# A hand-ordered attention and gated-MLP kernel: the same 8,030 operations replayed in another order

## The chip, the core and the metric

The kernel runs on one core of a Trainium2 chip. The metric is the device time of one execution in microseconds (us). Three runs of the kernel before took 676.34, 678.39 and 679.76 us; the median, 678.39 us, is the time before. A separate profiled execution took 677.01 us, and its trace is the source of every other time here.

## What is computed

The input is one sequence of 2048 rows of 512 numbers. The reference, cut to what matters:

```python
xn = _layernorm(x)                                   # x: (1, 2048, 512)
qkv = (xn @ wqkv).reshape(B, S, 3, 32, 16)           # 32 heads of 16
p = softmax(q @ k.T * 16 ** -0.5)                    # per head, 2048 x 2048
attn = (p @ v).reshape(B, S, D) @ wo
gate, up = xn @ W_gate, xn @ W_up                    # 512 -> 1792
mlp = (gate * (gate > 0) * up) @ W_down              # 1792 -> 512
out = x + attn + mlp
```

## The kernel before, in words

**Attention.** The scores of the 32 heads are taken in 32 blocks `(c4, gg, ee)`: 512 queries, a group of eight heads that fills the 128 partitions, and the even or odd four of those heads. A block has 16 key tiles, and each key tile has two units of 128x1024 scores: 1,024 units in all. For 704 of them ScalarE (ACT) takes the exponential out of PSUM into `ring` (L1664). The other 320 go two by two as 160 quads: VectorE (DVE) turns each of a quad's four 128x512 score tiles into int16 in `qd` (L1625), whose bits read as bf16 approximate an exponential, and GpSimd (POOL) adds two constants to it (L1639) to make two shifted copies. PE then multiplies the probabilities with `v_aug`, the values with columns of ones beside them, so that the sums of the softmax come out as further rows of the same product.

**The chain of the softmax sums** (`normalise`, L1477) runs 16 times: for 15 pairs of blocks (even and odd heads) and for block 30 alone; block 31 has its own ending. DVE copies the product out of PSUM (L1487, `o_sb`). A DMA gathers the rows of sums into `rsum` (L1505 and L1511, 8 KB). Four DMAs merge the odd heads into the even tile (L1519). DVE takes the reciprocal (L1526, `rrec`). Two DMAs scatter it into `rb` (L1528, 8 KB each). DVE spreads each row of `rb` over its head's rows (L1540, a shuffle, called "spread"), and multiplies (L1543, `x_sb<-o_sb,rb`).

**The rest** is put between the scores as background work: projections of q and k (the 15 later blocks of q leave DVE by L1094 and reach `qT` by eight DMAs each, L1100), gate and up with their weights streamed through two buffers (L1261), the down and output projections, and the stores of the rows (L1318).

**Tile positions on PE.** Most matmuls use one half of the array's rows (64 of 128) and are issued four at a time, 32 columns each. An operation on the other half can run beside it.

**What sets the order.** The program makes 8,030 operations, numbered as they are made, and puts them in no order itself. `ORDER` (L92) is a list of all 8,030 numbers, written out by a search done beforehand with a table of durations and rules; `SLOTS` (L409) lists which buffer or PSUM bank each of 3,024 tiles gets, in the same order. `Graph.follow` (L547) walks the list and appends each operation to its engine's queue (PE 5,586, DVE 985, ACT 719, SP 399, POOL 341). It adds the waits that the chosen buffers bring. `Graph.emit` (L583) makes semaphore waits from the dependencies. Each engine executes its queue strictly in that order, and a wait holds whatever stands behind it. Nearly all DMAs are issued by the SP queue: one instruction each, one after the other. Only the order within each engine's queue and the choice of buffers reach the chip.

**Numbers used below.** For the pair of blocks 10 and 11: 3344 is the copy to `o_sb` (L1487), 3345 the DMA to `rsum` (L1511), 3346 to 3349 the merging DMAs (L1519), 3350 the reciprocal (L1526), 3351 and 3352 the two DMAs to `rb` (L1528), 3353 the spread (L1540), 3354 the multiplication (L1543).

Of the kernel before, what the change touches and what calls it, by code (L numbers as in the profile page):

```python
# [102 lines left out]
    351, 166, 160, 541, 542, 164, 467, 263, 162, 354, 546, 547, 167, 264, 350, 352, 543, 348, 260, 266, 549, 271, 550, 548, 261, 272, 259, 267, 353, 268,  # L103
    468, 442, 554, 555, 551, 556, 270, 274, 355, 349, 356, 575, 576, 577, 275, 552, 273, 424, 428, 269, 276, 426, 580, 581, 284, 282, 484, 592, 593, 475,
    582, 594, 485, 279, 361, 545, 287, 277, 476, 477, 598, 553, 599, 600, 290, 283, 544, 281, 601, 602, 191, 286, 189, 280, 527, 292, 278, 285, 578, 193,
    606, 603, 607, 608, 187, 289, 609, 610, 611, 528, 33, 379, 359, 190, 300, 192, 186, 293, 188, 194, 636, 291, 637, 297, 288, 595, 638, 301, 639, 640,
    486, 488, 579, 427, 429, 490, 425, 294, 644, 645, 641, 646, 304, 492, 306, 596, 520, 656, 657, 310, 489, 519, 597, 491, 493, 299, 308, 487, 494, 661,
    662, 658, 663, 298, 307, 305, 680, 681, 295, 664, 665, 311, 309, 312, 534, 302, 532, 296, 303, 685, 686, 682, 687, 538, 536, 317, 315, 688, 689, 690,
    535, 539, 604, 537, 533, 683, 540, 319, 666, 667, 693, 694, 605, 613, 313, 714, 715, 695, 716, 668, 669, 316, 314, 320, 318, 321, 328, 719, 720, 642,
    322, 670, 326, 671, 684, 324, 722, 721, 723, 724, 337, 335, 329, 333, 325, 659, 323, 691, 327, 330, 673, 672, 729, 334, 730, 732, 733, 583, 612, 336,  # L110
    338, 585, 332, 377, 378, 614, 360, 376, 384, 386, 357, 358, 588, 331, 339, 731, 590, 737, 738, 734, 739, 717, 584, 380, 586, 660, 740, 741, 383, 589,
    587, 591, 381, 725, 783, 784, 780, 781, 742, 782, 718, 726, 643, 692, 727, 728, 799, 615, 382, 800, 801, 785, 389, 786, 395, 387, 385, 388, 804, 805,
    806, 396, 647, 651, 394, 392, 823, 824, 787, 788, 652, 393, 391, 654, 650, 828, 829, 825, 830, 674, 390, 397, 676, 648, 789, 678, 790, 362, 735, 849,
    850, 851, 649, 364, 617, 363, 677, 807, 808, 675, 679, 653, 655, 854, 855, 452, 736, 446, 448, 744, 809, 810, 450, 857, 858, 856, 859, 827, 453, 811,
    812, 447, 743, 862, 863, 459, 802, 451, 449, 454, 455, 865, 866, 813, 814, 860, 462, 852, 864, 867, 460, 881, 882, 883, 884, 885, 458, 861, 853, 886,
    887, 461, 900, 901, 457, 902, 501, 826, 868, 499, 456, 905, 498, 906, 463, 803, 869, 500, 870, 502, 504, 510, 908, 909, 907, 910, 888, 889, 505, 503,
    506, 935, 936, 937, 195, 792, 815, 816, 820, 509, 818, 513, 507, 890, 891, 511, 963, 964, 904, 965, 938, 512, 939, 508, 903, 911, 514, 515, 968, 969,
    749, 912, 940, 941, 747, 980, 981, 970, 982, 751, 798, 12, 942, 943, 794, 13, 791, 796, 745, 985, 986, 987, 944, 945, 821, 819, 750, 746, 817, 988,
    989, 1004, 1005, 1006, 752, 795, 990, 991, 797, 748, 753, 793, 1009, 1010, 1011, 966, 983, 558, 564, 560, 992, 993, 1012, 1013, 561, 559, 994, 995,
    946, 892, 947, 893, 822, 1017, 1018, 1014, 1019, 1008, 755, 563, 1020, 1021, 557, 967, 984, 1036, 1037, 562, 565, 1022, 1023, 950, 948, 569, 952, 567,  # L120
    873, 872, 1068, 1069, 1038, 1070, 1015, 573, 1007, 1024, 1025, 571, 1071, 1072, 1073, 1026, 1027, 1029, 566, 899, 570, 568, 897, 895, 871, 876, 1076,
    1077, 1078, 572, 574, 754, 758, 616, 621, 896, 898, 894, 619, 1095, 1096, 1079, 625, 623, 1080, 914, 874, 1081, 1082, 1039, 1100, 618, 1101, 624, 953,
    949, 951, 620, 622, 626, 1097, 1099, 1102, 1103, 1104, 1105, 1083, 1085, 1084, 1086, 1098, 1108, 1109, 1110, 1040, 999, 631, 633, 627, 629, 996, 997,
    1001, 913, 1003, 1139, 1140, 1107, 1129, 1130, 1131, 634, 1074, 1141, 1142, 1136, 1137, 1138, 630, 1002, 998, 1000, 628, 632, 635, 1143, 1144, 875,
    877, 1155, 1156, 1157, 958, 954, 1133, 956, 1075, 1016, 1160, 972, 960, 1161, 1106, 761, 878, 756, 879, 1087, 1088, 18, 1028, 1145, 1146, 1147, 880,
    1132, 1134, 975, 959, 1163, 1164, 1162, 1165, 977, 961, 971, 957, 973, 1195, 1196, 1197, 955, 962, 1034, 1030, 1032, 974, 976, 978, 979, 1214, 1215,
    1216, 700, 702, 696, 1031, 1033, 915, 1035, 698, 1236, 1237, 1238, 1198, 1199, 1159, 697, 1239, 1240, 701, 705, 1166, 703, 1217, 699, 704, 1158, 1244,
    1245, 1200, 1201, 711, 1241, 1246, 1094, 1092, 709, 707, 1090, 1202, 1203, 1263, 1264, 1265, 1089, 1093, 1204, 1205, 712, 1091, 1268, 1269, 706, 1247,
    1248, 708, 1242, 710, 713, 1271, 1272, 1270, 1273, 1063, 1065, 1167, 1243, 1059, 1249, 1250, 1061, 1206, 1276, 1277, 1278, 1218, 1251, 1252, 1062,
    1066, 1060, 1064, 1067, 1317, 1318, 1319, 766, 762, 764, 1253, 1254, 1267, 768, 1275, 1322, 1323, 757, 1279, 1280, 767, 1210, 1208, 763, 1281, 1282,  # L130
    1325, 1326, 769, 765, 770, 777, 773, 1324, 1327, 1330, 1331, 1148, 1150, 771, 1283, 1152, 1154, 1284, 775, 1349, 1350, 1332, 1351, 1285, 1286, 774,
    778, 1153, 776, 1149, 1151, 1354, 1355, 837, 1356, 772, 779, 1333, 1334, 1255, 1207, 1213, 1211, 835, 1209, 831, 1373, 1374, 833, 1335, 1336, 1212,
    1396, 1397, 836, 1337, 1338, 832, 1274, 1375, 1398, 834, 838, 839, 1399, 1400, 1401, 1288, 1287, 1377, 846, 844, 840, 1353, 1339, 1340, 842, 1329,
    1415, 1416, 845, 1357, 1358, 843, 1443, 1444, 1417, 1445, 847, 841, 848, 1352, 1266, 1359, 1360, 1186, 1403, 1448, 1449, 1450, 1189, 1376, 1191, 1193,
    1361, 1362, 1451, 1452, 1453, 1259, 1363, 1364, 1256, 1261, 1342, 1257, 1187, 1456, 1457, 1192, 1190, 1321, 1188, 1194, 1258, 1262, 1260, 1418, 1419,
    1497, 1498, 1458, 759, 760, 916, 1328, 1222, 1402, 1320, 1404, 1135, 1405, 1409, 1406, 1220, 1420, 1502, 1503, 1499, 1504, 1422, 1423, 1421, 1224,
    1521, 1522, 1523, 1219, 1225, 1294, 1292, 1290, 1223, 1221, 1424, 1425, 1526, 1527, 1528, 1500, 1226, 1227, 1231, 1232, 1289, 922, 924, 1293, 1291,
    1529, 1530, 1531, 1341, 918, 1459, 1460, 1366, 1365, 1427, 1429, 1534, 1461, 1462, 1535, 921, 919, 1346, 917, 1463, 1344, 1348, 1464, 1296, 1407,
    1553, 1554, 1536, 1555, 923, 1465, 1466, 1343, 1345, 920, 925, 1347, 1410, 1229, 1408, 1411, 1412, 1576, 1577, 1578, 927, 1228, 933, 1524, 931, 929,
    1454, 1505, 1506, 1295, 1588, 1589, 1590, 1557, 930, 1507, 1508, 928, 1593, 926, 1594, 1595, 932, 934, 1455, 1447, 1509, 1510, 1533, 1511, 1512, 1621,  # L140
    1622, 1446, 1428, 1432, 1426, 1430, 1626, 1623, 1627, 1628, 1537, 1525, 1539, 1538, 1645, 1646, 1041, 1647, 1043, 1625, 1372, 1045, 1370, 1468, 1368,
    1413, 1540, 1650, 1541, 1542, 1651, 1652, 1371, 1367, 1046, 1048, 1369, 1042, 1414, 1653, 1654, 1655, 1532, 1044, 1543, 1544, 1591, 1624, 1682, 1683,
    1596, 1501, 1597, 1047, 1049, 1433, 1431, 1701, 1057, 1702, 1556, 1469, 1684, 1703, 1053, 1598, 1599, 1473, 1729, 1730, 1470, 1600, 1601, 1474, 1052,
    1467, 1472, 1054, 1732, 1602, 1733, 1603, 1731, 1734, 1649, 1056, 1050, 1657, 1629, 1630, 1737, 1738, 1739, 1471, 1631, 1051, 1632, 1514, 1513, 1517,
    1515, 1519, 1055, 1058, 1756, 1757, 1758, 1516, 1436, 1518, 1520, 1633, 1634, 1761, 1762, 1592, 1438, 1635, 1636, 1434, 1656, 1798, 1799, 1648, 1658,
    1763, 1800, 1441, 1607, 1760, 1437, 1685, 1686, 1803, 1804, 1435, 1546, 1551, 1547, 1439, 1545, 1604, 1605, 1549, 1687, 1688, 1823, 1824, 1805, 1440,
    1442, 1552, 1117, 1550, 1548, 1115, 1828, 1829, 1825, 1830, 1611, 1689, 1690, 1609, 1113, 1736, 1122, 1112, 1831, 1832, 1126, 1691, 1692, 1694, 1111,
# [1572 lines left out]
```

## Time and profile before

| | |
|---|---|
| profiled execution | 677.01 us |
| span, first to last instruction | 675.2 us |
| granted TensorE clock | 1.000 |
| DVE busy | 591.8 us (88%) |
| POOL busy | 334.4 us (50%) |
| DMA moved | 28.65 MB, mean 42 GB/s |
| first exponential of the long unbroken run | 16.15 us |
| end of the last exponential | 665.17 us |

The profile counts an engine as busy from the start to the end of each instruction. PE's and ACT's instructions overlap their successors, so a busy share of 98 or 99% doesn't yet say which of the two sets the pace. "Idle before" is the time in which an engine had nothing running before an instruction, with what ended it. SPq rows are DMA issues on the SP queue: their duration is that of the issue, and the landing comes later. The line L485 is the helper that records every matmul of half the array, so those rows are told apart by their tiles.

### The profile page before, as it was taken

The page shows a single profiled execution, that of the slowest core. Times are in us where ns is not written, and L with a number is a line of the kernel's source. Part 1 is how long each engine was busy: PE and PEld are TensorE (multiplying, and loading weights), DVE is VectorE, ACT ScalarE, POOL GpSimd, SP SyncE. Part 2 cuts the span into 40 slices and gives each one's busy share as a digit, 9 for nine tenths or more (in the row PEclk, how much of TensorE's full clock was granted, in tenths as well). Part 3 has the DMA queues.
Part 4 walks back from the last instruction along what each step waited for, and adds up shares of the span by engine and source line. Part 5 has one row for each costly group of instructions (what it writes and reads, how often), then busy time and mean ns, then how long its engine had stood idle before and what let it go on. Part 6 is the DMA issues. An engine that isn't in the chain of part 4 may idle for free.

```text
span 675.2 us, 44161 instructions
## 1 busy us (share of the span) xinstructions
PE 665.6 (99%) x22348; PEld 364.4 (54%) x18916; DVE 591.8 (88%) x1001; ACT 658.5 (98%) x721; POOL 334.4 (50%) x345
## 2 busy tenths in 40 slices
PE   8999999999999999999999999999999999999997
PEld 3455555555554565545555555556554655555553
DVE  8958999998989788899999788999999967889886
ACT  7999999999999999989999999999999999999994
POOL 3200645553566555455556545664456653636540
PEclk9999999999999999999999999999999999999999
DMA  6330110122411020121201011020101012120001
GB/s 196 58 79 24 28 36 10 45 59 72 121 27 32 17 55 7 37 67 31 54 4 27 5 45 42 15 82 13 50 7 34 7 33 76 31 69 16 23 22 42
DMA packets 51472, 28.65 MB, mean 42 GB/s; under 512 B 18840, under 2 KB 50328, under 8 KB 51288
## 3 DMA queue, kind: packets, MB, share of 16 engines
q1 hardware_dynamic: 51144, 25.70, 14.6%
q8 instruction: 161, 2.64, 1.7%
q14 instruction: 23, 0.19, 0.1%
q10 hardware_dynamic: 144, 0.13, 0.1%
HBM read 18.22 MB, written 2.10 MB: 30 GB/s over the span
## 4 chain that ended last, share of the span: by engine, by line
PE 93%; ACT 3%; DVE 2%; DMA 1%; issue 0%; POOL 0%; SPq 0%
PE ps L485 93%; ACT ring L1664 3%; DVE stats L949 1%; DMA x_sb<-in_A_x_dram 0%; DVE xn_sb L972 0%; DMA rb<-rrec 0%; DVE qd L1625 0%; DVE xnT L1017 0%; PE ps L1398 0%; DVE mv L951 0%; DVE rb L1540 0%; DVE up_sb L1274 0%; ACT xn_sb L1438 0%; POOL rstd L933 0%; POOL rstd L947 0%
## 5 line engine op out<-in xcount | busy, mean ns | idle before, releaser
L1664 ACT ACTIVATE ring<-ps 128x1024 bf16<-128x1024 f32 x704 | 650.6, 1057 | 4.1 <-PE ps L485 3.5
L485 PE MATMUL ps<-qT,kT 64*32 64x512 bf16 x8192 | 468.4, 375 | 2.2 <-DVE qd L1625 1.6
L1639 POOL INT64_ADD qd<-qd x312 | 321.5, 1043 | 299.9 <-DVE qd L1625 145.6
L1625 DVE TENSOR_SCALAR qd<-ps 128x512 int16<-128x512 f32 x640 | 416.7, 684 | 44.5 <-PE ps L485 37.7
L485 PE MATMUL ps<-qd,v_aug 64*32 64x512 bf16 x3840 | 263.9, 375 | 0.1
L485 PE MATMUL ps<-ring,v_aug 64*32 64x512 bf16 x2816 | 230.0, 375 | 0.1
L1604 PEld LDWEIGHTS <-kT 64*32 64x32 bf16 x7152 | 154.1, 92 | 111.5 <-issue 20.8
L485 PE MATMUL ps<-xnT,wgs 64*32 64x512 bf16 x1792 | 136.6, 375 | 0.0
L1576 PEld LDWEIGHTS <-v_aug 64*32 64x32 bf16 x4264 | 102.7, 92 | 58.6 <-issue 12.8
L485 PE MATMUL ps<-xnT,wus 64*32 64x512 bf16 x1792 | 133.9, 375 | 0.0
L485 PE MATMUL ps<-Wd,hT 64*32 64x512 bf16 x768 | 64.4, 375 | 0.0
L1052 PEld LDWEIGHTS <-wus 64*32 64x32 bf16 x1792 | 43.3, 92 | 33.7 <-issue 7.4
L1052 PEld LDWEIGHTS <-wgs 64*32 64x32 bf16 x1792 | 43.2, 92 | 30.1 <-issue 6.3
L1052 PEld LDWEIGHTS <-hT 64*32 64x32 bf16 x1792 | 42.7, 92 | 29.9 <-issue 5.2
L485 PE MATMUL ps<-Wk,hT 64*32 64x512 bf16 x512 | 46.7, 375 | 0.0
L485 PE MATMUL ps<-Wv,hT 64*32 64x512 bf16 x512 | 45.5, 375 | 0.0
L1274 DVE COPY up_sb<-ps 128x512 f32<-128x512 f32 x56 | 38.4, 686 | 3.7 <-PE ps L485 3.1
L1278 DVE SCALAR_TENSOR_TENSOR hT<-ps,up_sb 128x512 bf16<-128x512 f32 x56 | 38.2, 683 | 2.9 <-PE ps L485 2.1
L485 PE MATMUL ps<-Wo_p,x_sb 64*32 64x512 bf16 x480 | 40.4, 375 | 0.2
L485 PE MATMUL ps<-xnT,Wq 64*32 64x512 bf16 x480 | 36.7, 375 | 0.0
L485 PE MATMUL ps<-xnT,Wk 64*32 64x512 bf16 x480 | 33.7, 375 | 0.8 <-DVE xnT L1017 0.8
L485 PE MATMUL ps<-Wv,xnT 64*32 64x512 bf16 x512 | 31.7, 375 | 0.5 <-DVE kT L1110 0.4
(81 smaller groups left out, 217.2 us busy)
## 6 DMA issues: line engine op xcount, KB each, us to landing
wgs<-in_B_W_gate_dram SPq DMA_DIRECT2D x38, 128.0 KB, 2.9
wus<-in_B_W_up_dram SPq DMA_DIRECT2D x38, 128.0 KB, 2.7
xr_sb<-in_A_x_dram SPq DMA_DIRECT2D x16, 128.0 KB, 2.4
qT<-qf SPq DMA_DIRECT2D x120, 16.0 KB, 2.2
o_sb<-o_sb SPq DMA_DIRECT2D x60, 32.0 KB, 2.5
out_dram<-xn_sb SPq DMA_DIRECT2D x15, 128.0 KB, 2.3
x_sb<-in_A_x_dram SPq DMA_DIRECT2D x8, 128.0 KB, 2.6
Wd<-in_B_W_down_dram SPq DMA_DIRECT2D x6, 128.0 KB, 2.8
```

Source lines behind the costliest of these rows:

```text
L485: return e.add_instruction(mybir.InstMatmult(name=e.bass.get_next_instruction_name(), engine=mybir.EngineType.PE, ins=[e.lower_ap(x), e.lo ...
L949: G.op("DVE", 580, lambda e, m=m: e.bn_stats(stats[:, m, :], xs(m)), reads=[t_xm[m]], writes=[t_st], prio=pr, order=last_xn if m == 4 and ...
L1052: e.ldweights(w()[rows, 32 * j:32 * j + 32], tile_position=(rows.start, 32 * j))
L1274: G.op("DVE", 603, lambda e: e.tensor_copy(up_sb[:, tup.slot, :], bank_of(tu)), reads=[tu], writes=[tup], prio=-590)
L1278: G.op("DVE", 603, lambda e: e.scalar_tensor_tensor(out=hT[:, th.slot, :], in0=bank_of(tg), scalar=0.0, in1=up_sb[:, tup.slot, :], op0=ALU ...
L1576: e.ldweights(vs(j), tile_position=(64 * half, 32 * j))
L1604: e.ldweights(ks(m), tile_position=(64 * half, 32 * m))
L1625: G.op("DVE", 601, lambda e, j=j, tx=tx: e.tensor_scalar(qd[:, tq.slot, 512 * j:512 * j + 512], ps[:, BANK[tx.slot], :], IBIAS[3], 0.0, op ...
L1639: G.op("POOL", POOL_NS, lambda e, x=x, n=n: e.int64_add(x().bitcast(I64), raw().bitcast(I64), SHIFTS[n + 1] * LANES), reads=[ti, tq, t_lib ...
L1664: exp_ops[u] = G.op("ACT", ACT_NS, lambda e, tr=tr, k0=k0: e.activation(ring[:, tr.slot, :, :], ps[:, 4 * k0:4 * k0 + 2, :], ACTF.Exp, sca ...
```

## The change

Only the two lists change. Both still hold 8,030 numbers and 3,024 slots, the set of numbers is the same, and the first 332 entries of `ORDER` and the first 93 of `SLOTS` are the same. The new list was searched with longer times in the search's table for the transfers of softmax sums, q and weights.

How far the queues differ, counted by sorting both lists into queues as `Graph.follow` does:

| queue | operations | first difference at place | operations at another place | mean shift, places |
|---|---|---|---|---|
| ACT | 719 | none | 0 | 0 |
| DVE | 985 | 86 | 259 | 0.36 |
| POOL | 341 | 22 | 243 | 1.3 |
| SP | 399 | 23 | 353 | 6.4 |
| PE | 5,586 | 169 | 4,522 | 5.6 |

In the queue of PE, neighbours on the same half of the array number 2,015 before and 2,034 after; an operation that finds its weights already loaded saves a load, and the loads number 4,702 before and 4,724 after.

For the 16 chains of softmax sums, the SP queue holds this many places from the last DMA to `rsum` to the first DMA to `rb`, and the DVE queue this many from the reciprocal to the spread (in the order of time):

| | chains 1 to 16 | sum |
|---|---|---|
| SP, before | 8, 9, 9, 4, 13, 8, 7, 6, 4, 6, 4, 11, 7, 5, 4, 4 | 109 |
| SP, after | 14, 7, 6, 5, 8, 2, 2, 4, 2, 4, 2, 3, 13, 7, 2, 4 | 85 |
| DVE, before | 11, 7, 12, 10, 23, 8, 11, 8, 9, 9, 12, 15, 8, 14, 4, 12 | 173 |
| DVE, after | 14, 11, 11, 9, 21, 10, 13, 8, 11, 8, 9, 12, 4, 8, 7, 22 | 178 |

The sixth chain (blocks 10 and 11) in the SP queue, operation numbers with their lines:

```
before, places 173 to 185
3346 L1519, 3349 L1519, 3345 L1511, 2726 L1100, 3155 L1100, 3347 L1519, 3348 L1519,
46 L911, 3159 L1100, 3163 L1261, 3352 L1528, 41 L911, 3351 L1528
after, places 173 to 185
3345 L1511, 3346 L1519, 3351 L1528, 3160 L1100, 3352 L1528, 3348 L1519, 3161 L1261,
40 L911, 3163 L1261, 3158 L1100, 3349 L1519, 3347 L1519, 3162 L1261
```

The diff replaces 305 lines of `ORDER` and the 22 lines of `SLOTS`; here are the first replaced line and, of the sixth chain, the lines with the reciprocal, the transfers to `rb` and the spread:

```diff
--- before.py
+++ after.py
@@ -100,335 +100,335 @@
...
-    351, 166, 160, 541, 542, 164, 467, 263, 162, 354, 546, 547, 167, 264, 350, 352, 543, 348, 260, 266, 549, 271, 550, 548, 261, 272, 259, 267, 353, 268,
...
-    3485, 3310, 3308, 2858, 3436, 3437, 3312, 2860, 3161, 3158, 3507, 3508, 3504, 3509, 3438, 3439, 3346, 3349, 3345, 3350, 2726, 3155, 3347, 2857, 3386,
...
-    2970, 3537, 3542, 3543, 3352, 2976, 3463, 2974, 3490, 3491, 3547, 3548, 3544, 3549, 3400, 3398, 41, 3351, 3153, 2544, 3353, 3068, 3404, 3402, 2972,
...
+    351, 166, 160, 541, 542, 164, 467, 263, 162, 354, 546, 547, 167, 264, 266, 350, 348, 352, 260, 543, 548, 442, 549, 550, 551, 468, 259, 355, 261, 267,
...
+    3397, 3399, 3502, 3503, 3504, 3350, 3351, 3160, 3352, 3348, 3161, 3308, 2860, 2862, 3310, 3436, 3312, 3437, 2857, 3507, 3508, 3309, 3438, 3311, 3439,
...
+    3366, 3370, 3368, 2976, 2972, 3547, 3548, 3490, 3491, 3353, 3544, 3549, 40, 3163, 3158, 3349, 3404, 3074, 3068, 3445, 3398, 3402, 3400, 2974, 3550,
...
```

More of the change, by code (lines that the diff above doesn't have):

```diff
@@ L429 @@
-    "31d20011102081310131310920121300415210601171300a21b0200e2021f0100001cd4101300621450010210112530e01f1060711703082012090001ab21104021321018034"
-    "2150232001220003c40201d30e9231f0062331731200312101a31b2412032313223014523080112120196201700c230410230de01f2004211005220101020202131060173083"
-    "00301900a321b00c331d001314541023103e0140f21221301031101101a1110b81094267150001111230")]
+    "0001213130200012110232110324115016720118009101a13b210c30210d311ef011012011103220313450108210961730011a100bc2100de1f301891001cd01673102132100"
@@ new lines @@
+    "11452301ab0300021110018930c0131120d21100023e31f00381010301014520060211007211ab90e21f0202031132401a0131450300123211110c301d140603011000073189"
+    "01302b310e1f130a1130040b21100303000113c014510c121d0003082210039113ad0be1314312320f61121702312103003211011408201e19203145100a31b223f022112312"
+    "01312cd010310ef13130001892312031206703201045002011g14302031302300110121cd0a0012230be22013h210f83413029003120003016101143074015100013123i0311"
+    "cd02330802130009e11041j00f101ab310003110306100417004101533003112300081131920c02141130de01f022001ab21063217021010031450423000123201c100110300"
@@ new lines @@
+    "d22102023803130096031200207a21b01042015110011324300ef00111231002189020a40120102b6170102014212312001145500211cd210e10421f1100a013b12300306613"
+    "00701101001001489203041013530217321003c31013010da01b1130e41213f100189330233012320630211320742321205032411310c231d320a313b20301231ef306113078"
+    "0013009411300504031121301c11d311013ab1031233133021ef32302081103120410961217102411150002211110a2110be21f1210413001231200c1d130631173041031510"
+    "30131118090311103e114010fa10121b002022313004c3031d008030119100630017304120231ab2000324110002021450120e01f3100031821029c303120d12322000602173"
@@ new lines @@
+    "3042015331e300f4013152100a311203b110130081301209c331012403d211ef1242011012031023120363210072251a120b831101930204041130100015c1d020e06101130f"
+    "0001130013120170304011389130201c1040d630103070081ab36004110005e111f30112030201842990002311016201122007212310c0201d00c221301ab010041ef1010082"
+    "11320942311d20501111006100170031020121310301132cd0802431901010031g10ef301331ab1304341150001170h011010c30d211332410120a31b10e11f0061321721108"
+    "219102314102510112001043120c0d232130322a130be21f324210163207003213310142123150033189001004011cd10231310013062117301131ab0312131454103c1d101e"
@@ new lines @@
+    "031010f031103061017003124302001232020a21b002281020941150010221c000de1001f20102103201003116722000a111000b2101203080221943031210c231d1003011ef"
+    "01034102113052211003021310a44123311b106231103207411013015182350910201ef31001cd104100013122030121370111a212001b600171042291104520011341ef2010"
+    "1cd0a0101820921031310001101112120161b13110740151100e00113000f31ab100420312189001e10cd001310330013401221330f000401105000167130013g890240011ef"
+    "311021ab1020c11d3231001h310110214510022313230623i3124100782110090211311401411j3510e323210020101f3123010a1b3300c131d00006311240007432111005e3"
@@ new lines @@
+    "1f11003a1b32100c301d041030383190003202311302213220133e120f321167300412143205c213020d831920a0231b000212040011212304321105121611207a1110b81019"
+    "421203001111210c21d100e21f1202011013314530a11b06041700c1113d1002214301e1f0011010101801112090212000034015012410602317030201ef020101a220b01112"
+    "14201c01d10002010131210403120305167130a0013300be141f001300103180030190001120061611101207c3110d83019300134712330051100ab0010160300742135820c3"
+    "1d1320e1141f20102322103019231230411083119230c12300d4215320632172330a01210be43211020f2321100380210119103010110a00111430001b167001ef130c11d300"
@@ L435 @@
+    "1321110314512031112330111ef041330a22131101010b61170301890040104167521301ef0010113120")]
 LOG2E = 1.4426950408889634
```

19 lines of the change are left out of this document (removed), and 604 rows, old and new, of the table ORDER.

## The prediction

> **What bounds the kernel now.** I read the page first: busy shares and the costliest groups.
>
> ```profile
> PE 665.6 (99%) x22348; PEld 364.4 (54%) x18916; DVE 591.8 (88%) x1001; ACT 658.5 (98%) x721; POOL 334.4 (50%) x345
> ...
> L1664 ACT ACTIVATE ring<-ps 128x1024 bf16<-128x1024 f32 x704 | 650.6, 1057 | 4.1 <-PE ps L485 3.5
> ```
>
> PE and ACT both look full. For PE the timeline corrects that: two streams, one on each half of the array.
>
> ```profile
> 281.87 0.38 PE L485 MATMUL ps<-qd,v_aug 64*32 64x512 bf16 x4
> 282.03 0.38 PE L485 MATMUL ps<-xnT,wus 64*32 64x512 bf16 x4
> 282.08 0.38 PE L485 MATMUL ps<-qd,v_aug 64*32 64x512 bf16 x4
> 282.25 0.38 PE L485 MATMUL ps<-xnT,wgs 64*32 64x512 bf16 x4
> 282.30 0.38 PE L485 MATMUL ps<-ring,v_aug 64*32 64x512 bf16 x4
> ```
>
> Each stream starts four matmuls every 0.215 us (281.87, 282.08, 282.30), so both start eight. The page's 22,348 matmuls need 22,348 / 8 x 0.215 = 601 us of the 675: PE has some 10% to spare if its halves alternate well. ACT's exponentials overlap (1,057 ns each, begun more often), so I take their period from the timeline.
>
> ```profile
> 275.60 12.10 ACT L1664 ACTIVATE ring<-ps 128x1024 bf16<-128x1024 f32 x13
> 289.55 2.86 ACT L1664 ACTIVATE ring<-ps 128x1024 bf16<-128x1024 f32 x3 [1.86 <-PE ps L485]
> ```
>
> Thirteen took 12.10 us: (12.10 - 1.06) / 12 = 0.920 us each. Three took 2.86: (2.86 - 1.06) / 2 = 0.90, the quickest I can show. The windows, counting exponentials alone, say whether this pace is kept:
>
> ```profile
> 200.00:276.00 76.00, 75.89 (x83) 1.00 0.12 29
> 276.00:294.00 18.00, 16.14 (x18) 1.00 0.23 60
> 294.00:400.00 106.00, 105.99 (x116) 1.00 0.11 28
> ```
>
> ACT is idle 0.1 us of 76 and 0.01 of 106, and 1.86 us between 276 and 294. The list of exponentials sets the time, and the order of operations can give back only what ACT loses: one real hole, and the difference between 0.92 and 0.90.
>
> **The hole.** The chain of waits through it:
>
> ```profile
> 282.93 0.61 DVE up_sb L1274
> 283.54 0.14 SPq L1528
> ...
> 284.24 1.85 DMA rb<-rrec
> ...
> 286.12 0.73 DVE rb L1540 x2
> ...
> 287.48 0.69 DVE qd L1625
> ```
>
> The spread waits for a transfer to `rb`, and behind it on DVE stands the eviction of a score tile (287.48). PE waits for that:
>
> ```profile
> 286.25 0.38 PE L485 MATMUL ps<-qd,v_aug 64*32 64x512 bf16 x4
> 288.22 0.38 PE L485 MATMUL ps<-qT,kT 64*32 64x512 bf16 x4 [1.59 <-DVE qd L1625]
> ```
>
> and ACT for PE (the 1.86 us above). Why was the transfer late? DVE's rows and the SP queue's:
>
> ```profile
> 279.16 0.34 DVE L1526 RECIPROCAL rrec<-rsum 128x32 f32<-128x32 f32 x1
> ...
> 286.12 0.01 DVE L1540 LOAD_MASK_SELECT rb<-rb  x1 [1.99 <-DMA rb<-rrec]
> ```
>
> ```profile
> 276.65 0.60 SPq L1511 DMA_DIRECT2D rsum<-o_sb  x1
> 277.30 1.74 SPq L1100 DMA_DIRECT2D qT<-qf  x2
> 279.08 1.23 SPq L1519 DMA_DIRECT2D o_sb<-o_sb  x2
> 280.35 0.58 SPq L911 DMA_DIRECT2D Wo_l<-in_A_wo_dram  x1
> 280.98 0.51 SPq L1100 DMA_DIRECT2D qT<-qf  x1
> 281.52 1.52 SPq L1261 DMA_DIRECT2D wgs<-in_B_W_gate_dram  x1
> 283.09 0.59 SPq L1528 DMA_DIRECT2D rb<-rrec  x1
> 283.73 0.47 SPq L911 DMA_DIRECT2D Wo_l<-in_A_wo_dram  x1
> 284.24 0.60 SPq L1528 DMA_DIRECT2D rb<-rrec  x1
> ```
>
> The reciprocal is done at 279.50. The transfers start at 283.09 and 284.24, since the SP queue is issuing other DMAs, about 0.6 us each. The transfer itself takes 1.85. So 4.7 us are lost in the queue and 1.9 in the transfer.
>
> **The change, part by part.**
>
> *The sixth chain of sums.* In the new SP queue, from the table above, the transfers to `rb` stand at places 175 and 177, behind one DMA to `rsum` and one merging DMA, with one q DMA between. They can start as soon as the reciprocal ends: 0.6 + 0.6 for the two issues ahead of the second, + 1.85, about 3.1 us after the reciprocal's end. The spread stays at place 433 of DVE while the reciprocal moves from 425 to 423, so nine instructions of about 0.6 us (before: seven) lie between: 5.4 us. 5.4 against 3.1: the wait goes, with 2.3 us to spare. ACT gets back its 1.86 us, and nothing later absorbs it, since ACT is busy to the end of its list. The least would be 0 (another wait stands at the same place), the most the DVE's 1.99. I take **-1.9**.
>
> *What waits because of this.* SP must now stand at place 175 until the reciprocal ends. Behind it are q DMAs and weight loads which before were issued from 277.30 to 283.09. Their own time to landing is short:
>
> ```profile
> wgs<-in_B_W_gate_dram SPq DMA_DIRECT2D x38, 128.0 KB, 2.9
> ```
>
> Over all chains the new queue has 85 places between sums and scatter instead of 109: the same trade, 24 DMAs moved behind. If none of them is late, it costs 0; a weight that is late by all of one landing costs 2.9. No row gives their leads, but in the list of waits no matmul of L485 waits for a DMA, so every lead is positive now; an SP operation moves by 6.4 places on average, some 4 us at 0.6 each, both ways. I take 0 and keep 2.9 a place for the range.
>
> *A new tight place.* At the thirteenth chain the DVE distance falls from 8 to 4. There DVE isn't packed:
>
> ```profile
> 563.51 0.69 DVE L1625 TENSOR_SCALAR qd<-ps 128x512 int16<-128x512 f32 x1 [1.14 <-PE ps L485]
> 565.04 0.69 DVE L1625 TENSOR_SCALAR qd<-ps 128x512 int16<-128x512 f32 x1 [0.84 <-PE ps L485]
> ```
>
> Three instructions at this spacing (565.04 - 563.51 = 1.53 us) are 4.6 us, more than the 3.1 needed; packed at 0.6 they are 1.8, and the wait is 1.3. Between 0 and 1.3 I take **+0.3**.
>
> *PE's order.* No matmul is added. Neighbours on one half rise by 19, loads by 22. A load lasts 92 ns:
>
> ```profile
> L1604 PEld LDWEIGHTS <-kT 64*32 64x32 bf16 x7152 | 154.1, 92 | 111.5 <-issue 20.8
> ```
>
> If each new neighbour left the other half empty for one of the two streams' 0.215 us, that would be 19 x 0.215 = 4.1 us of one half. That is spread over 675 us in which PE has 10% to spare; only what falls just ahead of a score reaches ACT. Between 0 and 4.1 I take **+0.4**. The Trainium skill, page "TensorE: Matmul & The Clock Gate", section "Part 3: Packing small matmuls — row/col tiling", says a weight load runs under matmuls only when it goes to another row group; by that rule each of the 19 would show its load, 19 x 92 ns = 1.7 us instead of my 0.4, and the sum would be 1.3 higher. The row of 92 ns doesn't say whether loads are covered.
>
> *The small rest.* 259 places of DVE and 243 of POOL change by 0.36 and 1.3 on average: no mean gain or loss, only scatter, and I take 0. Prologue and ending keep their operations.
>
> **Sum:** 677.0 (the profiled execution's own time) - 1.9 + 0.3 + 0.4 = 675.8. The median of the runs shown is 678.4, 1.4 above the profiled execution; I forecast between 675.8 and 677.2: **676.5 us**.
>
> **The rivals.** Differences under 0.5% (3.4 us) are about what can't be told from no change here.
>
> *A, the forecast (0.43):* hole gone, little given back: 674 to 679.
>
> *B, a larger gain (0.10):* with no transfer late, the fine order also brings more exponentials from 0.92 to 0.90. Over 350 of them that is 7 us at most, 4 with half of it: 676.5 - 4 = 672.5 down to 670. For: DVE is only 88% busy. Against: new neighbours on one half are no fewer.
>
> *C, slower (0.20):* the SP queue holds. SP stands at the scatter until the reciprocal is done, in 16 places; from the point where this standing outlasts the lead of the next weight or q transfer, PE stands at the first matmul that reads it, up to 2.9 us each. Three such places: 676.5 + 3 x 2.9 = 685; two 682. For: 353 of 399 SP operations move, by 6.4 places on average. Against: SP's 399 issues of 0.6 us fill 240 us of 675, so its backlog is local.
>
> *D, no effect (0.15):* at the sixth chain another wait ends just as late (the multiplication, which POOL waits for, moves from place 434 to 441): 677 to 679. The Trainium skill, page "DMA: Bandwidth & Descriptors", section "Issuing engines are not separate DMA queues", calls the sequencer's time to start a DMA usually small beside the DMA; by that rule moving a DMA ahead in SP earns little. The rows above contradict it here: 4.7 us of queue against 1.85 of transfer.
>
> *E, slower by scatter (0.12):* PE's queue shifts by 5.6 places (0.6 us at 0.1075 each) against DVE's 0.36. Where an eviction now comes after PE wants its bank, PE waits. Twelve places of 0.6 us: 676.5 + 7 = 684. For: at 288.22 PE did wait for such an eviction. Against: it is the only one that the windows above show.
>
> **How the numbers follow.** Faster by over 0.5% (under 675.0): B and the lower quarter of A, 0.22. Slower by over 0.5% (over 681.8): C and E less their mildest, 0.30. The rest, 0.48. The range from 672.5 to 684.5 leaves out the lower part of B and the upper parts of C and E, some 2 in 10; A's own is 674 to 679.
>
> **What would show it.** Right: no idle time of the spread at a transfer to `rb` in the sixth chain; ACT idle under 0.3 us between 276 and 294; exponentials ending near 663.5. C is right if PE's weight loads or scores wait for a DMA to `wgs`, `wus` or `qT`; E if PE's idle time behind L1625, L1274 or L1487 grows above its 1.6 us; the term for PE's order is wrong if the windows of 100 us hold fewer exponentials than now without any idle time. The prediction fails if a hole of over 3 us stands anywhere in ACT's list.

## The result, and the profile after

| | before | after |
|---|---|---|
| median (7 runs each) | 676.71 us | **673.87 us** |
| lowest to highest | 676.08 to 679.76 | 673.03 to 675.08 |
| ratio to before, 95% interval | | 0.9955 [0.9941, 0.9969] |
| profiled execution (span) | 677.01 (675.2) us | 673.03 (671.1) us |

The change makes the kernel 0.45% faster, some 3 us. The interval excludes "no change". The ratio lies just inside the half per cent that the prediction called "the same", and the interval reaches across that line. The profiled executions differ by 4.0 us. Part of that is a before that was profiled 0.3 us above its median and an after 0.8 us below its own. What follows is made of the traces, one execution of each kernel, so it explains 4.0 us where the medians show 3.

First the page of after, with the same two rows as before: busy shares, and the exponentials in the costliest groups.

```profile
PE 663.5 (99%) x22348; PEld 360.3 (54%) x19004; DVE 592.4 (88%) x1001; ACT 657.4 (98%) x721; POOL 334.0 (50%) x345
...
L1664 ACT ACTIVATE ring<-ps 128x1024 bf16<-128x1024 f32 x704 | 649.5, 1056 | 1.5 <-PE ps L485 1.1
```

DVE and POOL work as long as before, PE and ACT 1 to 2 us less, the weight loads (PEld) 4.1 us less although there are 88 more of them; these busy times count overlapping work and name no cause yet. ACT's idle time at PE fell from 3.5 to 1.1 us. The windows with the exponentials alone say where. Of before, then of after (start and end, length, ACT busy with the number begun, clock, DMA share, GB/s):

```profile
116.00:216.00 100.00, 99.91 (x109) 1.00 0.22 60
...
276.00:294.00 18.00, 16.14 (x18) 1.00 0.23 60
...
16.00:661.00 645.00, 641.56 (x695) 1.00 0.15 38
```

```profile
116.00:216.00 100.00, 100.00 (x110) 1.00 0.23 61
...
276.00:294.00 18.00, 18.00 (x20) 1.00 0.21 53
...
16.00:661.00 645.00, 644.22 (x699) 1.00 0.15 38
```

Between 276 and 294 ACT now begins 20 exponentials instead of 18 and is never idle: the hole is gone. Over the whole stretch it begins four more, and its idle time falls from 645 - 641.56 = 3.44 us to 0.78. The hole gave 1.86 of the 2.66 so won; the remaining gain of ACT is spread thin.

The end of the last exponential is at 644.60 + 20.58 = 665.18 in before and 639.18 + 22.19 = 661.37 in after:

```profile
644.60 20.58 ACT L1664 ACTIVATE ring<-ps 128x1024 bf16<-128x1024 f32 x22
```

```profile
639.18 22.19 ACT L1664 ACTIVATE ring<-ps 128x1024 bf16<-128x1024 f32 x24
```

So 3.8 of the 4.1 us of span are won in ACT's list, and the ending is 0.3 us shorter. Read from the start of each of the 704 exponentials, after minus before is -0.1 us at exponential 64, -0.6 at 192, -0.9 at 288, **-2.8 at 320**, -3.2 at 448 and -3.8 at the last. That is one step of -1.9, and a gradual gain (below: the slope) of about -1.9 over the rest.

The sixth chain on DVE in after (start, duration, then idle time before in brackets with what ended it):

```profile
276.81 0.34 DVE L1526 RECIPROCAL rrec<-rsum 128x32 f32<-128x32 f32 x1
...
283.52 0.01 DVE L1540 LOAD_MASK_SELECT rb<-rb  x1
283.52 0.74 DVE L1540 STREAM_SHUFFLE rb<-rb 128x512 f32<-128x512 f32 x1
```

and on the SP queue:

```profile
273.34 0.60 SPq L1511 DMA_DIRECT2D rsum<-o_sb  x1
273.99 0.52 SPq L1519 DMA_DIRECT2D o_sb<-o_sb  x1
277.18 0.59 SPq L1528 DMA_DIRECT2D rb<-rrec  x1
277.82 0.51 SPq L1100 DMA_DIRECT2D qT<-qf  x1
278.37 0.59 SPq L1528 DMA_DIRECT2D rb<-rrec  x1
```

The spread has no idle time before it any more. The reciprocal ends at 277.15, SP issues the first scatter 0.03 us later and the second at 278.37, and the spread comes at 283.52. Note also the gap in SP's rows: after the merging DMA (273.99 + 0.52 = 274.51) SP **stands** until 277.18, 2.67 us, because the next DMA in its queue needs the reciprocal. That this costs nothing here is not self-evident, as the first experiments show.

The thirteenth chain, where the prediction saw a new tight place:

```profile
556.67 0.34 DVE L1526 RECIPROCAL rrec<-rsum 128x32 f32<-128x32 f32 x1
...
560.63 0.01 DVE L1540 LOAD_MASK_SELECT rb<-rb  x1 [0.20 <-DMA rb<-rrec]
```

It is tight, by 0.20 us, and in the waits of after no DVE instruction waits longer than that for a scatter. PE's one wait for an eviction, 1.6 us in before, is gone: in the list of waits of after no matmul waits for `qd`, `up_sb` or `o_sb` of DVE.

### The profile page after: what moved, and what is told of

Read it like the earlier page. It is cut to its first block, busy times and chain, and to the rows that moved or that the text cites. A ratio compares the mean times of both kernels' runs of the same rounds, so it can differ in the third digit from the quotient of the medians.

```text
span 671.1 us, 44261 instructions
## 1 busy us (share of the span) xinstructions
PE 663.5 (99%) x22348; PEld 360.3 (54%) x19004; DVE 592.4 (88%) x1001; ACT 657.4 (98%) x721; POOL 334.0 (50%) x345
## 4 chain that ended last, share of the span: by engine, by line
PE 87%; ACT 9%; DVE 2%; DMA 0%; issue 0%; POOL 0%; DVEq 0%
PE ps L485 87%; ACT ring L1664 9%; DVE stats L949 1%; DVE xn_sb L972 0%; DMA x_sb<-in_A_x_dram 0%; DVE xnT L1017 0%; DVE xn_sb L1442 0%; DVE mv L951 0%; DVE up_sb L1421 0%; DVE o_sb L1419 0%; DVE o_sb L1416 0%; DVEq L723 0%; POOL rstd L933 0%; POOL rstd L947 0%; DVE qT L1209 0%
## 5 line engine op out<-in xcount | busy, mean ns | idle before, releaser
L485 PE MATMUL ps<-qT,kT 64*32 64x512 bf16 x8192 | 464.9, 375 | 0.4 <-ACT qT L1208 0.2
L1625 DVE TENSOR_SCALAR qd<-ps 128x512 int16<-128x512 f32 x640 | 416.6, 684 | 42.1 <-PE ps L485 37.4
L485 PE MATMUL ps<-qd,v_aug 64*32 64x512 bf16 x3840 | 264.4, 375 | 0.0
L485 PE MATMUL ps<-ring,v_aug 64*32 64x512 bf16 x2816 | 225.8, 375 | 0.0
L485 PE MATMUL ps<-xnT,wgs 64*32 64x512 bf16 x1792 | 137.4, 375 | 0.0
L485 PE MATMUL ps<-xnT,wus 64*32 64x512 bf16 x1792 | 134.3, 375 | 0.0
L1576 PEld LDWEIGHTS <-v_aug 64*32 64x32 bf16 x4252 | 101.9, 92 | 56.6 <-issue 10.3
L485 PE MATMUL ps<-Wd,hT 64*32 64x512 bf16 x768 | 66.5, 375 | 0.0
L485 PE MATMUL ps<-Wk,hT 64*32 64x512 bf16 x512 | 46.2, 375 | 0.0
L485 PE MATMUL ps<-Wv,hT 64*32 64x512 bf16 x512 | 44.9, 375 | 0.0
L485 PE MATMUL ps<-Wo_p,x_sb 64*32 64x512 bf16 x480 | 40.5, 375 | 0.1
L485 PE MATMUL ps<-xnT,Wk 64*32 64x512 bf16 x480 | 35.3, 375 | 0.8 <-DVE xnT L1017 0.8
L485 PE MATMUL ps<-xnT,Wq 64*32 64x512 bf16 x480 | 35.7, 375 | 0.0
L485 PE MATMUL ps<-Wv,xnT 64*32 64x512 bf16 x512 | 32.2, 374 | 0.5 <-DVE kT L1110 0.4
```

Source lines behind the costliest of these rows:

```text
L485: return e.add_instruction(mybir.InstMatmult(name=e.bass.get_next_instruction_name(), engine=mybir.EngineType.PE, ins=[e.lower_ap(x), e.lo ...
L1576: e.ldweights(vs(j), tile_position=(64 * half, 32 * j))
L1625: G.op("DVE", 601, lambda e, j=j, tx=tx: e.tensor_scalar(qd[:, tq.slot, 512 * j:512 * j + 512], ps[:, BANK[tx.slot], :], IBIAS[3], 0.0, op ...
```

## The experiments

Each experiment's lists are written on fewer lines, so their line numbers are 47 lower than those of before and after: L1578 is L1625, L1493 is L1540, L1481 is L1528, L438 is L485, and so on. The expectations name the runs as they were made: e1 is experiment 1, e7 is 2, e6 is 3, e10 is 4, e5 is 5, e3 and e4 are 6a and 6b, e11 and e13 are 7a and 7b, and e8, e9 and e12 are 8a, 8b and 8c. Each was timed in five rounds beside before on the same chip. Where one list's order is changed, the buffers stay as that list had them. The **offset** at an exponential is its start in one run minus its start in the trace of before. "Interval" below is the time from the start of one exponential to the start of the next; 0.903 us is the quickest steady one. A **hole** is an interval over 1.3 us, and what it has above 0.903 is its loss; what all other intervals have above 0.903 together is the **small loss** (both are sums over the starts in the one profiled execution of each run, from the sixth exponential on).

**1. Is the late scatter alone the cause?** In before, the two DMAs to `rb` go right behind the last gathering DMA; nothing else moves.

```diff
 SP queue, places 175 to 186
-3345 rsum, 2726 qT, 3155 qT, 3347, 3348, 46 Wo, 3159 qT, 3163 wgs, 3352 rb, 41 Wo, 3351 rb, 3153
+3345 rsum, 3351 rb, 3352 rb, 2726 qT, 3155 qT, 3347, 3348, 46 Wo, 3159 qT, 3163 wgs, 41 Wo, 3153
```

> The list of before with two numbers moved: the two DMAs to rb of the sixth chain (3351, 3352) stand right behind the one to rsum in the SP queue, places 176 and 177 instead of 185 and 183. Theory (their place in the SP queue made the hole): the spread no longer waits for a transfer, ACT is idle under 0.3 us between 276 and 294 us, and the time falls by 1.9 us, a ratio near 0.997 to before. Rival (another wait stands just behind): 0 to -0.5 us.

Measured: 677.33 us against 676.25, ratio 1.001 [0.9999, 1.0022]. No gain. The spread's wait is gone, but ACT's hole only moved, from exponential 298 to 294 (ACT is idle 1.11 us there instead of 1.86). The SP queue of this experiment, then PE's rows:

```profile
276.53 0.60 SPq L1464 DMA_DIRECT2D rsum<-o_sb  x1
279.81 1.19 SPq L1481 DMA_DIRECT2D rb<-rrec  x2
281.04 1.21 SPq L1053 DMA_DIRECT2D qT<-qf  x2
```

```profile
283.18 0.38 PE L438 MATMUL ps<-xnT,wgs 64*32 64x512 bf16 x4
284.71 0.62 PE L438 MATMUL ps<-qT,kT 64*32 64x512 bf16 x12 [1.15 <-DVE up_sb L1227]
```

SP stands from 277.13 to 279.81 and only then issues 2726, the q DMA, at 281.04 where before issued it at 277.30. The score that reads this q starts at 284.71. The profile puts its wait down to a DVE copy, but DVE's row shows that this had long been done:

```profile
283.13 0.68 DVE L1227 COPY up_sb<-ps 128x512 f32<-128x512 f32 x1
```

It ended at 283.81, 0.9 us before. What came just before 284.71 is the q transfer: 2726 lands at 284.65, 3.6 us after its issue. The queue of before had a reason: ahead of the scatter stood a q DMA with a nearer need.

**2. The same trade, taken back in after.** 2726 goes from place 159 of the SP queue to place 182, behind the scatter; the rest is after.

```diff
 SP queue of after, places 157 to 183
-2742, 2775, 2726 qT, 2780, ... 3345 rsum, 3346, 3351 rb, 3160 qT, 3352 rb, 3348, 3161 wus, 40 Wo, 3163 wgs, 3158 qT, 3349
+2742, 2775, 2780, ... 3345 rsum, 3346, 3351 rb, 3160 qT, 3352 rb, 3348, 3161 wus, 40 Wo, 3163 wgs, 3158 qT, 2726 qT, 3349
```

> The list of after with the one q DMA 2726 moved back from place 159 to 182 of the SP queue, behind the transfers to rb. Theory: it is issued near 282 us, lands 1.8 to 3.6 us later, and the score that reads it, at 282.5 us, waits 2 to 3 us: a hole of that size in ACT, ratio to before 0.9985 to 1.000 against 0.9955 for after. Rival (SP's order matters only for the sums): no hole, 0.9955.

Measured: 675.58 against 676.22, ratio 0.9992 [0.9981, 1.0003], where after had 0.9955: most of the gain is lost by moving one 16 KB DMA. ACT's timeline of this experiment, the chain of waits there, and the SP queue's row with 2726, the second of the two:

```profile
286.57 13.91 ACT L1617 ACTIVATE ring<-ps 128x1024 bf16<-128x1024 f32 x15 [2.44 <-PE ps L438]
```

```profile
282.14 0.61 DVE qd L1578
282.75 2.46 issue
285.21 6.97 PE ps L438 x232
```

```profile
282.76 1.15 SPq L1053 DMA_DIRECT2D qT<-qf  x2
```

The chain calls it "issue", time in which the profile shows no releaser. 2726 is issued at 283.31 and lands at 285.15; at 285.21 the first score that reads its rows begins. Beside after, exponential 295 starts 0.10 us later and the next one 2.57 us later, and that stays for the next 300. So after closed the hole with **two** moves: the scatter ahead, and 2726 far ahead of it (in after it is issued at 247.12, lands at 248.91, and is first read at 282.48).

**3. Both moves in before.** 2726 goes ahead of the wait as well.

```diff
 SP queue of experiment 1, places 169 to 179
-3027, 3154 qT, 3161, 3158, 3346, 3349, 3345 rsum, 3351 rb, 3352 rb, 2726 qT, 3155 qT
+3027, 2726 qT, 3154 qT, 3161, 3158, 3346, 3349, 3345 rsum, 3351 rb, 3352 rb, 3155 qT
```

> The list of before with three numbers moved in the SP queue: the two DMAs to rb right behind the one to rsum (places 177 and 178), as in e1, and the q DMA 2726 from place 176 to 170, ahead of the wait of 3154 (SP stands there from 253 to 272 us). Theory (in e1 the hole moved to the score that reads this q DMA, which SP's standing at rb had pushed from 277.3 to 281.0 us): with both early the hole goes, ACT idle under 0.3 us between 276 and 294, and the time falls by 1.9 us, ratio 0.997 to before. Rival (POOL's adds behind the multiplication, or an eviction, hold PE at the same place): 0 to -0.6 us.

Measured: 676.13 against 676.22, ratio 1.000 [0.9991, 1.0009]. Across the old hole the offset goes from +0.45 to -1.47 us, which is the 1.9 in full; then 0.9 us is lost again in the interval behind exponential 304, and by exponential 384 it is 1.15 us. ACT's timeline and the end of the chain of waits:

```profile
269.59 24.09 ACT L1617 ACTIVATE ring<-ps 128x1024 bf16<-128x1024 f32 x26
294.44 5.72 ACT L1617 ACTIVATE ring<-ps 128x1024 bf16<-128x1024 f32 x6 [0.76 <-PE ps L438]
```

```profile
280.62 0.55 SPq L1481
281.17 0.04 issue
281.21 0.57 SPq L1053
...
289.45 0.59 SPq L1262
290.04 0.04 issue
290.09 2.96 DMA wus<-in_B_W_up_dram
293.05 0.05 issue
293.10 7.02 PE ps L438 x203
```

From the scatter at 280.62 to the weight load at 290.09 the chain is SP's own issues, one behind the other without a pause: the standing has made the SP queue itself the path, and the next victim is a weight.

**4. And the weight too.** That load (3162, `wus`) goes right behind the scatter.

```diff
 SP queue of experiment 3
-3351 rb, 3352 rb, 3155 qT, ...
+3351 rb, 3352 rb, 3162 wus, 3155 qT, ...
```

> As e6 (the list of before with the two rb DMAs and the q DMA 2726 earlier), and one weight load more: 3162 (W_up) stands right behind the rb DMAs, place 179. In e6 the hole went, but the first matmul that reads this load waited at 293.1 us. Theory (SP's queue holds: each transfer moved ahead makes the next one in line late, until all that are due have been moved): now -1.9 us against before, ratio 0.997. Rival (the next in line, a q DMA or W_gate, is late in its place): 0 to -1 us, with a wait for that DMA in the list.

Measured: 675.88 against 675.96, ratio 0.9996 [0.9986, 1.0005]. In the trace the step across the hole is now -1.4 us (the offset goes from +0.3 to -1.1) and it stays. What is left of the hole, 0.6 us, is made by a merging DMA, which the moved ones pushed back and for which a multiplication on DVE waits:

```profile
283.75 1.94 DMA o_sb<-o_sb
...
285.77 0.69 DVE x_sb L1496
```

But the time hardly moved. The trace's gain of 0.9 us of span and the medians' 0.1 do not fit; before's own profiled execution lay above its median in these sessions (677.01 against 676.0 to 676.3), which covers about that much. How much of the hole an average execution of before pays isn't settled by this pair. So the theory of this experiment holds for the trace and not for the time. Experiment 2 against after is the better measure of what such a hole costs: by the ratios 0.37% or 2.5 us, with intervals that don't touch; by the medians, which were taken in different sessions, 1.7 us.

**5. Could the spread simply come later?** In before, spread and multiplication move three DVE instructions back.

```diff
 DVE queue, places 432 to 438
-3491 qd, 3353 spread, 3354 mul, 3493 qd, 2977 hT, 3511 qd, 3075 up
+3491 qd, 3493 qd, 2977 hT, 3511 qd, 3353 spread, 3354 mul, 3075 up
```

> The list of before with the spread and the multiplication of the sixth chain (3353, 3354) three instructions later in DVE's queue (433 to 436); the SP queue as before, so the transfers to rb are as late as before. Theory (what costs is not the late transfer but what stands behind the waiting spread on DVE): three evictions of 0.6 us go ahead of the wait, which falls from 2.0 to 0.2 us or less, and the time by 1.6 to 1.9 us, ratio 0.997. Rival (the late transfer itself costs, through POOL or the output projection): 0.

Measured: 676.75 against 676.25, ratio 1.0003 [0.9991, 1.0014]. The spread doesn't wait; PE does, first for an eviction and then for POOL:

```profile
289.63 0.38 PE L438 MATMUL ps<-qT,kT 64*32 64x512 bf16 x4 [1.31 <-DVE up_sb L1227]
290.24 0.38 PE L438 MATMUL ps<-qd,v_aug 64*32 64x512 bf16 x4 [0.23 <-POOL qd L1592]
```

The two moved instructions (1.4 us) now stand ahead of an eviction and of POOL's addition, and PE wants both. The hole moves to exponential 300 and keeps most of its size (an interval of 2.72 us instead of 2.94).

**6. Which engine's order made the slope?** First the SP queue alone is exchanged, in both directions. 24 and 17 of the 399 places are not as in the other list, where a cycle of waits would have stood otherwise.

```diff
 experiment 6a: PE, DVE, POOL, ACT and buffers of before
-SP queue of before
+SP queue of after
 experiment 6b: PE, DVE, POOL, ACT and buffers of after
-SP queue of after
+SP queue of before
```

> PE, DVE, POOL and ACT in the order of before with its buffers; the SP queue in the order of after (375 of its 399 places exactly, the rest off by a few). Theory (the hole is a matter of the SP queue, the gradual other 2 us of after come from the order on PE): -1.9 us, ratio 0.997. Rival (all of the gain comes from the transfers' order): -3.8 us in the span, ratio 0.9945 to 0.9955.

> PE, DVE, POOL and ACT in the order of after with its buffers; the SP queue in the order of before (382 of 399 places exactly). Theory: the hole at the sixth chain comes back (the spread waits 1 to 2 us for rb) and the gradual 2 us stay: some 2 us below before, 2 above after, ratio 0.997. Rival (all from the transfers): no difference from before, ratio 1.000.

Measured: 685.51 against 676.25, ratio 1.0128 [1.0106, 1.0151] for 6a, and 684.58, ratio 1.0105 [1.008, 1.013] for 6b. Neither theory nor rival came out: both are slower than either parent, by holes. The waits of 6a, then of 6b (total, times, longest):

```profile
ACT ring L1617 <- PE ps L438: 11.8, 16, 4.6
DVE x_sb L1496 <- DMA o_sb<-o_sb: 6.7, 2, 3.9
```

```profile
ACT ring L1617 <- PE ps L438: 11.0, 12, 2.1
DVE rb L1493 <- DMA rb<-rrec: 9.3, 5, 2.9
```

In 6a multiplications wait for merging DMAs, in 6b spreads for scatters. Neither SP order fits the other list's engines. The small loss, though, goes with the engines and their buffers, and not with SP:

| PE, DVE, POOL and buffers of | SP of | holes, us | small loss, us |
|---|---|---|---|
| before | before | 2.0 | 15.6 |
| before | before, edited (experiments 1, 3, 4) | 2.2, 1.3, 0.6 | 15.7, 15.8, 15.9 |
| before | after (6a) | 10.3 | 16.3 |
| after | after | 0 | **13.9** |
| after | after, edited (experiment 2; 0.8 of the holes lies at exponential 647, far from the edit) | 3.4 | 13.4 |
| after | before (6b) | 10.8 | 14.3 |

It is 13.4 to 14.3 us with after's engines and 15.6 to 16.3 with before's. So the slope comes with the orders of PE, DVE and POOL or with the buffers, which were exchanged along with them: 1,665 of the 3,024 tiles lie in another buffer in after, among them 624 of the 704 of `ring`. No run exchanges the buffers alone. One number of the page goes the same way: the loads' busy time is 364.4 us in before and 364.2 in 6a, 360.3 in after, 360.4 in experiment 2 and 361.4 in 6b, so loads overlap each other more in the new list. That is no price by itself: 8c below has 360.3 as well and is 3% slower.

**7. Which of the three?** DVE's and POOL's orders are exchanged between the lists, with the PE order of the other (in 7a 251 and 240 operations change place; 7 operations of PE in 7a and 48 in 7b move with them, against cycles of waits).

```diff
 experiment 7a: PE, ACT and SP of after
-DVE and POOL queues of after
+DVE and POOL queues of before
 experiment 7b: PE, ACT and SP of before
-DVE and POOL queues of before
+DVE and POOL queues of after
```

> PE, ACT and SP in the order of after with its buffers (7 PE operations differ); DVE and POOL in the order of before (251 and 240 operations move). ACT's small losses (intervals of 0.90 to 1.30 us, summed above 0.903) are 13.9 us in after and 15.6 in before. Theory (they come from the order on PE): 13.9 stays within 0.5, ratio to before 0.9945 to 0.9965 unless a hole opens. Rival (from DVE and POOL): 15.6, ratio 0.998.

> The mirror of e11: PE, ACT and SP in the order of before with its buffers (48 PE operations differ), DVE and POOL in the order of after. Theory (order on PE): small losses stay at 15.6 within 0.5, and the hole stays, since SP is as before: ratio 1.000 to 1.003. Rival (order on DVE and POOL): small losses 13.9, ratio 0.9975.

Measured: 764.72 against 675.96, ratio 1.1304 [1.1284, 1.1325] for 7a and 770.37, ratio 1.1391 [1.1376, 1.1407] for 7b, far outside every expectation. The waits of 7a:

```profile
ACT ring L1617 <- PE ps L438: 75.7, 87, 3.4
PE ps L438 <- DVE qd L1578: 36.3, 45, 2.6
...
PE ps L438 <- POOL qd L1592: 14.7, 16, 3.0
```

A mean shift of 0.36 places in DVE's queue and 1.3 in POOL's looked like nothing; put against the PE order and the buffers of the other list it costs 13%. The question can't be answered this way, since the three orders do not come apart, and they were not taken apart from the buffers either.

**8. Is it late scores?** Another reading of the slope: some exponentials have to wait for a late score. An exponential reads two scores; called late here is one whose second score PE starts 0.4 us or more after the end of the exponential that frees its bank. Counted in the traces, before has 63 such exponentials, with 6.7 us of small loss, and after 37 with 4.6. If they are the cause, bringing late scores forward on PE should win more, and putting them back should lose. Three experiments, with an example of each edit in PE's queue (the score pair is marked):

```diff
 8a, after: 91 late pairs one to four places earlier
-277, 193, 191, 283, 545, [598], 192, [599]
+277, [598, 599], 193, 191, 283, 545, 192
 8b, before: 106 late pairs earlier
-468, 442, [554, 555], 270
+468, [554, 555], 442, 270
 8c, after: 223 pairs two places later
-354, [546, 547], 264, 266, 350
+354, 264, 266, [546, 547], 350
```

> The list of after; 91 of the 704 pairs of scores for ACT, those that in after's trace began over 0.30 us after the exponential that frees their bank and whose exponential then came late, stand 1 to 4 places earlier in PE's queue (158 places in all). Nothing else moves. Theory (the many small losses of ACT are scores that stand too far back on PE): of the 8.8 us that after loses at these 91, a third to a half goes, -3 to -4 us against after, ratio to before 0.990. Rival (PE is simply full there, and the work passed over makes the next scores late): 0 to -1 us, ratio 0.994 to 0.9955; if the evictions of passed-over work come late, slower.

> The same edit on the list of before: 106 pairs of scores stand 1 to 6 places earlier on PE (206 places in all), among them the pair at the hole (unit 298). Theory: -4 to -6 us, ratio 0.991 to 0.994 to before. Rival (PE is full there): 0 to -1 us, with the hole still in place.

> The opposite of e8: in the list of after, the 223 pairs of scores that began within 75 ns of the exponential that frees their bank, so that PE may have stood waiting for it, stand two places later on PE, and two other operations go first. Theory (what costs PE is standing at a score; other work fits there): the small losses fall from 13.9 to 11-12 us, ratio to before 0.991 to 0.994. Rival (as in e8, any move of scores upsets what DVE and POOL have been timed to): small losses above 16, ratio 1.000 or more.

Measured: 683.49 against 676.22, ratio 1.0108 [1.0094, 1.0122] for 8a; 685.91, ratio 1.0142 [1.0128, 1.0156] for 8b; 697.23 against 675.96, ratio 1.031 [1.0296, 1.0324] for 8c. The small loss rises from 13.9 to 21.1 in 8a, from 15.6 to 22.6 in 8b and to 35.3 in 8c. Later is bad, and earlier is bad too. The theory in its simple form fell: a late score is where the loss shows, but moving scores alone mends nothing. Why is open. A score brought forward pushes back what it overtakes, and that may be late in its turn. But the edits also part operations that shared loaded weights: the pages count 188 more load instructions in 8a than in after, 264 more in 8b than in before, and 572 more in 8c than in after. The slowdowns of 9.6, 9.7 and 23.4 us by the medians are 0.04 to 0.05 us for each of them, so the loads fit as well, and no run holds them fixed. The list of waits of 8a has no large wait of ACT to point at, only small ones:

```profile
ACT ring L1617 <- PE ps L438: 5.0, 16, 1.3
```

## Why the prediction was right, and where it wasn't

The forecast was 676.5 us, in a range from 672.5 to 684.5, with "within 0.5%" the likeliest. Measured were 673.87 and 0.45% faster. The range held, and it is four times as wide as the change. By the forecast's own lines the result came out between two rivals, under the 675.0 where "faster" began and just under the 674 where A's own range did. Against its middle the forecast was 2.6 us too slow. Its sum for the trace, 675.8, missed the profiled 673.03 by 2.8 us, and one step carries 2.3 of that. The 0.7 us that was added for the median came out about right by luck: it rested on three runs of before, whose median of 678.39 became 676.71 with seven, while after's median happens to lie 0.84 us above its own profiled execution.

**The hole (-1.9): right in size, incomplete in its reason.** ACT's list won 1.9 us between exponentials 288 and 320. The prediction had the spread 5.4 us and the scatter 3.1 us behind the reciprocal; the second scatter was issued 1.2 us behind it, which with the 1.85 that a transfer took in before is the 3.1, and the spread came 283.52 - 277.15 = 6.4 us behind it, so the margin was 1 us larger than estimated. But the step said that the scatter's earlier place wins this by itself. Experiments 1, 3, 4 and 5 each remove the spread's wait from before, and none is faster. The scatter's place was one of several things that had to fit: the q DMA 2726 and the weight 3162 must be out of the way too. In after they are: 2726 is issued 30 us earlier than in before, and 3162 at 284.09 instead of 288.59. The prediction costed the moved DMAs by their mean shift and didn't look up the one that stood behind the wait. That the 1.9 came in whole was luck as far as its reasoning goes.

**The standing of SP (0, up to 2.9 a place, rival C).** The mechanism is real: SP stands 2.7 us at the scatter both in experiment 1 and in after. In experiment 1 it made a q transfer late and gave the gain back; in after it made no hole. The term's value of 0 was right for after, and rival C's 0.20 was not too much: moving 2726 by 23 places makes a wait of C's kind in after, 2.5 us in the trace. "Every lead is positive now" was too weak an argument to exclude it, as a lead says nothing until the first read of each transfer is looked up in the trace.

**The tight place (+0.3).** It was 0.20 us of wait on DVE, and none of it is seen on ACT: from exponential 448 to 608 the offset stays between -3.1 and -3.2.

**PE's order (+0.4) is the step that failed**, together with "the small rest" that was taken as 0. Neighbours on one half rose by 19 and loads by 22, and the prediction made a loss of them. The small loss fell instead, by 1.8 us (15.64 to 13.87), and the table of experiment 6 ties that to the orders of PE, DVE and POOL with their buffers. Counting neighbours and loads over the whole list gave the wrong sign here: with more loads their busy time fell and the kernel got faster. How many operations move is no price either: experiment 8a moves 358 of PE's operations where the change moved 4,522, and loses nearly 10 us against after. Whether a load has a price of its own stays open, as experiment 8 shows. The Trainium skill, page "TensorE: Matmul & The Clock Gate", section "Part 3: Packing small matmuls — row/col tiling", would have put the sum 1.3 us higher still; no run here isolates a load, and no such loss shows in the total.

So the sum, with each term as the two traces have it, is 677.0 - 1.9 (hole) - 1.9 (slope) - 0.3 (the ending) = 672.9 beside the profiled 673.03. This only divides up the difference between the traces and tests nothing. Exponentials end at 661.4 and not at 663.5 as forecast.

**The rivals.** B, more exponentials nearer 0.90 us, happened in small: 1.8 us where it had priced 4 to 7. D's rule from the Trainium skill, page "DMA: Bandwidth & Descriptors", section "Issuing engines are not separate DMA queues", that the time to start a DMA is usually small beside the DMA, speaks of one DMA, and the traces don't contradict that: in experiment 2, 2726 takes 0.59 us to issue and lands 1.84 us after its issue begins. What the prediction drew from it, that moving a DMA ahead in SP earns little, is what fails: 23 places in SP's queue cost 2.5 us there, since the issues ahead of a DMA and SP's standing add up. E, scatter between PE and DVE, is what the mixed lists of experiment 7 show at full size; in after PE waits for no eviction.

**What stays open:** which of the three orders makes the slope, or whether the buffers do. The exchange of DVE and POOL destroys the fit before it can tell, and moving scores alone made it worse. Nor did any edit of before reach after, so the list as a whole is shown to be better. Only the hole has a shown cause, and that from one side: one DMA put back in after reopens a hole and costs most of the gain, while closing most of the hole in before (experiment 4) didn't show in its time.

## What to carry to other kernels

Before moving a DMA ahead in an in-order queue, look up what it waits for and what stands behind it: the queue stands for as long as that wait lasts, and it costs as soon as that outlasts the lead (the time between landing and first read) of a transfer behind it. If a hole is closed by one edit, look for it again in the exponentials around it before you count the gain; here it moved to a q transfer, then to a weight, then to a merge. And don't price a re-ordered list by averages (mean shift, neighbours, loads): here they gave the wrong sign. Orders of several engines that were searched together fell apart here when they were mixed (1 to 14% slower).

## What the runs showed of the hardware that was not expected

A small DMA lands hardly sooner than one eight times its size. From the page of after (KB each, median us from issue to landing), then from that of before, whose row for `wgs` (2.9) the prediction shows:

```profile
wgs<-in_B_W_gate_dram SPq DMA_DIRECT2D x38, 128.0 KB, 2.5
...
qT<-qf SPq DMA_DIRECT2D x120, 16.0 KB, 2.4
o_sb<-o_sb SPq DMA_DIRECT2D x60, 32.0 KB, 2.5
```

```profile
qT<-qf SPq DMA_DIRECT2D x120, 16.0 KB, 2.2
o_sb<-o_sb SPq DMA_DIRECT2D x60, 32.0 KB, 2.5
```

In after 16, 32 and 128 KB land within 0.1 us of each other, in before within 0.7 us. And a wait's named releaser can be wrong when a transfer ends it: in experiment 1 the score's wait was put down to a copy that had ended 0.9 us earlier, and in experiment 2 to no one at all; the DMA that ended both was found only by following what the matmul reads.
